# Two attentions on one core: the wait of a split maximum moves into the matmul itself, and row loads go two a step

## The chip, the core and the metric

The kernel runs on one core of a Trainium2 chip. The metric is the device time of one execution in microseconds (us), the median of several runs; lower is better. A core has a matrix engine (PE in the profile; its weight loads are listed apart as PEld), a vector engine (DVE), a scalar engine (ACT), a general engine (POOL), and SP, which here only issues DMA transfers. Each engine takes its instructions in the order in which the program lists them for it, and waits for others through semaphores.

## The reference

Two independent attention layers on inputs of 2048 rows and 576 columns, 32 heads of 18 columns each, results side by side. B, the second, is full softmax attention and makes up nearly all the work; A, the first, looks only at 8 earlier rows (0, 2, ... 14 back).

```python
S, D, H, Dh = 2048, 576, 32, 18
qkv = (x @ wqkv).reshape(S, 3, H, Dh)               # for A and for B
# B: every row against every row
scores = einsum("hqd,hkd->hqk", q, k) * Dh ** -0.5
out_B = einsum("hqk,hkd->hqd", softmax(scores), v) @ wo
# A: row s against rows s, s-2, ..., s-14
logits = where(idx >= 0, einsum("hsd,hswd->hsw", q, k[idx]) * Dh ** -0.5, -1e9)
out_A = einsum("hsw,hswd->hsd", softmax(logits), v[idx]) @ wo
```

## The kernel before, in words

First, up to about 420 us, both projections are computed and stored to DRAM; B's queries and keys go to `dqk`, split into a high and a low part for accuracy. Then the main loop does B's attention while POOL works through A between the lines.

B's heads are taken in 8 groups of 4. For each group, the queries (`qs`) and keys (`ks`) of the four heads are laid into one of three sets of SBUF tiles, so that two heads can share the array: one head stands on partitions 0 to 63 (row group 0), its neighbour on 64 to 127 (row group 1). Matmuls on different row groups run side by side. The softmax needs each row's largest score before the exponential, so every score is computed twice: once, ahead of time, for its row maximum (`take`, line 239; DVE reduces it on lines 256, 258 and 272 into `mx`), and once transposed for the exponential (`score`, line 388; ACT makes the exponentials `e` and `ee` on lines 398 and 401). The maxima of a block go through a small chain (`least`, `turn`, `halve`, `order`, `place`) and through DRAM (`dm`, lines 300 and 306) into two extra rows of `qs`.

The main loop has 512 steps: 8 groups, 4 blocks of 512 queries, 16 blocks of 128 keys. A step's instructions on PE are in a fixed order. In a plain step, `PLAIN = "D1AzwE2B"` gives it, one letter for one matmul:

- `D` and `E`: the two halves (256 columns each) of a maximum in two parts. `D` is on row group 0, `E` on row group 1, and both write into the same bank of PSUM, which one reduction (line 272) then empties. `first_part` issues `D` and hands back a function that issues `E`.
- `A` and `B`: whole maxima (512 columns) on row groups 0 and 1.
- `1` and `2`: scores of heads 1 and 2, on row groups 1 and 0, each in a bank of its own, each emptied by one ACT instruction on line 398.
- `z` and `w`: scores of heads 3 and 0, on row groups 1 and 0, into a tile of two banks (`pair`), emptied by one ACT instruction on line 401.

After these eight, `weigh` (line 870) multiplies the exponentials of the step before with the values into `po`: four matmuls that the profile lists as eight, on all 128 rows of the array. About one step in fifteen also holds products of A's output (line 1211); its order is then made by `in_turn`.

Banks are handed out in turn from two rings: two banks for `1` and `2`, three for `D`, `A` and `B`. So `2` waits until ACT has emptied the bank of the last `2`, and `B` until DVE has emptied the bank of the last `B`.

`E` must not begin while `D` still writes into the bank that they share. Line 267 sees to that: an instruction that does nothing (`nop`) is put ahead of `E` and made to wait for `D`'s semaphore. With `nofuse=True` it stays an instruction of PE's queue.

Transfers are issued by SP from an agenda: `plan(start, pieces)` enters functions under step numbers, and each step runs its own (`due`). For each group from the fourth on (g = 3 to 7), line 1328 enters the twelve loads of the next set of rows (`stack_loads`: six for `qs`, line 216, then six for `ks`, line 215; 288 KB each), from step 64 (g - 2) + 1 on. Other transfers of the same queue lie among them: the maxima (`dm`), the denominators of the softmax (`den`, `drec`, `rec`, lines 904 to 907), the results (`do`, line 900), and for A the rows (`akv`, `aq`, line 996) and the finished attention (`at`, `ahl`, lines 1090 and 1092) that the products of line 1211 read.

Of the kernel before, what the change touches and what calls it, by code (L numbers as in the profile page):

```python
# [33 lines left out]
STEPS = NB * NT  # L34
# [29 lines left out]
def rows(t, *dims):  # L64

    return bass.AP(tensor=t.tensor, offset=t.offset, ap=[list(d) for d in dims])
# [3 lines left out]
def two_attentions(ctx: ExitStack, tc, xa, wa, woa, xb, wb, wob, out):  # L70
# [5 lines left out]
    nc = tc.nc  # L76
# [18 lines left out]
    def bank(kind=None):  # L95
        r = rings[kind or ring]
        n = min((i for i in r if i not in held), key=lambda i: freed[i]) if ring == "pool" else r[0]
        if ring != "pool":
            r.append(r.pop(0))
        t = (p_bank if n < 5 or projecting else p_pair).tile([128, 512], F32, name=f"bank{n}")  # L100
        if not projecting:
            held[n] = t
        return t
# [53 lines left out]
    def filled(r, ns, t=None):  # L157

        n = held_as(t)
        busy[r] = max(busy[r], 0 if n is None else freed[n] + 165) + ns  # L160

    def emptied(engine, ns, r, t):

        busy[engine] = max(busy[engine], busy[r] + 214) + ns
        n = held_as(t)
        if n is not None:
            del held[n]
            freed[n] = busy[engine] + 100
# [6 lines left out]
    def split_on(engine, hi, lo, raw):  # L175
        engine.tensor_copy(hi, raw)
        engine.tensor_sub(lo, raw, hi)
# [5 lines left out]
    def later(n, f):  # L183
        agenda[step + n].append(f)

    def plan(start, pieces):
        for n, f in pieces:
            agenda[start + n].append(f)
# [18 lines left out]
    def stack_loads(g, *pieces, issue=load):  # L207
        qs, ks = (t.bitcast(F32) for t in sets[g % 3])

        def part(t, base, n, r, i, d, m):  # L210

            at = 64 * r + DH * n + d
            first = dqk[i, base + DH * (4 * g + r) + d]
            if t is ks:
                return lambda: issue(ks[at : at + m], rows(first, (S, m), (2 * DH * S, 2), (1, S)))
            return lambda: issue(qs[at : at + m], rows(first, (S, m), (512, NB), (2 * DH * S, 2), (1, 512)))

        return [part(t, base, n, r, i, d, m) for t, base, parts in ((qs, 0, (0, 0, 1)), (ks, D, (0, 1, 0)))
                for d, m in pieces or ((0, DH),) for n, i in enumerate(parts) for r in range(2)]


    def behind_of(later, *before):

        for b in before:
            tc.add_manual_dep(later.ins, b.ins.name,
                              mybir.DependencyInfo(mybir.DependencyClass.Sync, mybir.DependencyReason.DATA),
                              reason="in order")

    def block(g, b):

        qs, ks = sets[g % 3]
        mx = maxes.tile([128, 2, 2, 4, 6], F32, name="mx", bufs=3)
        left = 2 * 8 * 6
        rest = [[(k, t, p) for k in range(NB) for t in range(4) for p in range(2)] for _ in range(2)]

        def take(ps, r, k, t, p, at, n):

            rows_ = slice(64 * r, 64 * r + 54)
            return nc.tensor.matmul(ps, qs[rows_, b, p, 128 * t : 128 * t + 128],  # L239
                                    ks[rows_, p, 512 * k + at : 512 * k + at + n], start=True, stop=True)  # L240

        def made(n):
            nonlocal left
            left -= n
            if left == 0:
                later(int(projecting), least)

        def whole(r):
            k, t, p = rest[r].pop(0)
            ps = bank()  # L250
            take(ps, r, k, t, p, 0, 512)
            filled(r, 226, ps)

            def reduce():
                if k < 2:
                    nc.vector.tensor_reduce(mx[:, r, p, t, k : k + 1], ps, axis=AX.X, op=ALU.max)  # L256
                else:
                    nc.vector.tensor_reduce(mx[:, r, p, t, 2 * k - 2 : 2 * k], ps.rearrange("q (h n) -> q h n", h=2),  # L258
                                            axis=AX.X, op=ALU.max)
                emptied("DVE", 598, r, ps)  # L260
                made(1 + (k > 1))

            return reduce

        def part(i, k, t, p, r, ps, before=None):
            if before:
                behind_of(nc.tensor.nop(nofuse=True), before)
            ins = take(ps[:, 256 * r : 256 * r + 256], r, k, t, p, 256 * i, 256)
            filled(r, 120, None if before else ps)

            def reduce():
                nc.vector.tensor_reduce(mx[:, :, p, t, 2 * k - 2 + i], ps.rearrange("q (h n) -> q h n", h=2),  # L272
                                        axis=AX.X, op=ALU.max)
                emptied("DVE", 598, r, ps)
                made(2)

            return ins, reduce

        def least():
            m = least_rooms[n_least[0] % 2]  # L280
            n_least[0] += 1
            nc.vector.tensor_reduce(m[:, :16], mx.rearrange("q r p t k -> q (r p t) k"), axis=AX.X, op=ALU.max,
                                    negate=True)
            later(1, lambda: turn(m))

        def turn(m):

            parts = maxes.tile([128, 2, 32], F32R, name="mt", bufs=2)
            raw = parts[:, 1].bitcast(F32)
            nc.vector.transpose(raw, m)  # L290
            later(1, lambda: halve(parts, raw))

        def halve(parts, raw):
            split_on(nc.gpsimd, parts[:, 0], parts[:, 1], raw)
            later(1 if g == NG - 1 else 2, lambda: order(parts))

        def order(parts):

            for k in range(2):
                load(rows(dm[g, b, k, 0, 0], (32, 4), (128, 32), (1, 32)), parts[:, k].bitcast(F32))  # L300
            later(1 if g == NG - 1 else 3, place)

        def place():
            placed.add((g, b))
            for k in range(2):
                load(qs.bitcast(F32)[54 + k : 128 : 64, b].rearrange("r p n -> r (p n)"),
                     dm[g, b, k, :16].rearrange("(r i) n -> r (i n)", r=2))

        return rest, whole, part
# [198 lines left out]
    with (tc.tile_pool(name="x", bufs=1, side="right") as xp,  # L508
# [103 lines left out]
        if True:  # L612
# [195 lines left out]
            for k in range(2, 14):  # L808
                n = 46 if k == 2 else 36 + 4 * k
# [7 lines left out]
            def leave_a(c, b, n, ps):  # L817
                o = xp.tile([128, 512], F32, name="ohi", bufs=4)
                nc.scalar.activation(o[:n], ps, AF.Copy)  # L819
                load(da[128 * c : 128 * c + n, HALO + 512 * b : HALO + 512 * b + 512], o[:n])  # L820
# [18 lines left out]
            for c, b in order:  # L839
                n = min(128, 3 * D - 128 * c)  # L840
                work_list.append(((b % 2, ws[c][0], xas[b][0], slice(0, n), every),
                                  lambda ps, n=n: ps[:n], lambda ps, c=c, b=b, n=n: leave_a(c, b, n, ps)))
# [417 lines left out]
    def first(t, b, h):  # L1260
        sums[t, b, h] = bank()
        for c in range(4):
            some(sums[t, b, h][:, :288], t, h, c, *olds[b][c], c == 0, False)
# [44 lines left out]
    def partial(t, h):  # L1308

        b = NB - 1  # L1310
        if h == 0:
            name = ("aq", "ao", "aohi")[t]
            ys["part", t] = work.tile([128, DH, SUB], F32, name=name, bufs=1)
        y = ap(ys["part", t], (1, DH * SUB))[:, 288 * h : 288 * h + 288]
        waiting.append(lambda: alone(*sum_of(y, t, h, olds[b])))
        sums[t, b, h] = (y,)
# [8 lines left out]
        plan(A_FROM + GAP * j, local(j))  # L1325
    for g in range(1, NG):
        if g > EARLY:
            plan(STEPS * (g - 2) + 1, [(n, f) for n, f in enumerate(stack_loads(g))])
        if g == NG - 1:
            plan(STEPS * g, [(4, lambda: fetch_old(0)), (24, lambda: fetch_old(1)), (34, lambda: fetch_old(3)),  # L1330
                             (36, lambda: fetch_old(2))])
            plan(STEPS * g, [(n, lambda t=t, h=h: partial(t, h)) for n, (t, h) in
                             zip((40, 41, 42, 44, 46, 48), [(t, h) for t in range(3) for h in range(2)])])
            plan(STEPS * g, [(62, lambda: outside.append(lambda: first(3, NB - 1, 0)))])
            for b in range(NB - 1):
                producing.update(STEPS * g + NT * (b + 1) + (31 if b == 0 else 7) + n for n in range(8))
        plan(STEPS * (g - 1), [(24, lambda g=g: load_v(g))])
# [19 lines left out]
    while step < ALL:  # L1357
        n, kt = divmod(step, NT)
        g, b = divmod(n, NB)
# [84 lines left out]
```

## Time and profile before

| | |
|---|---|
| time, median of 3 runs | 1599.24 us (1596.97 to 1600.29) |
| the profiled execution | 1598.7 us, its span 1596.8 us |
| granted clock of PE | 0.999 of full speed |
| PE busy | 1586.8 us, 99% of the span |
| DVE, ACT, POOL busy | 88%, 74%, 60% |
| reductions of maxima in two parts (line 272) | 478 |
| loads of rows issued by SP for g = 3 to 7 | 60, of 288 KB |

The span runs from the first to the last instruction. Start times below count from its start. Records of matmuls overlap: one can begin before its weights are all loaded, and the ends are modelled. Weight loads have records of their own, and a matmul's wait for a semaphore stands at its weight load. The records of an instruction that only waits are not counted as busy.

### The profile page before, as it was taken

The page shows a single profiled execution, that of the slowest core. Times are in us where ns is not written, and L with a number is a line of the kernel's source. Part 1 is how long each engine was busy: PE and PEld are TensorE (multiplying, and loading weights), DVE is VectorE, ACT ScalarE, POOL GpSimd, SP SyncE. Part 2 cuts the span into 40 slices and gives each one's busy share as a digit, 9 for nine tenths or more (in the row PEclk, how much of TensorE's full clock was granted, in tenths as well). Part 3 has the DMA queues.
Part 4 walks back from the last instruction along what each step waited for, and adds up shares of the span by engine and source line. Part 5 has one row for each costly group of instructions (what it writes and reads, how often), then busy time and mean ns, then how long its engine had stood idle before and what let it go on. Part 6 is the DMA issues. An engine that isn't in the chain of part 4 may idle for free.

```text
span 1596.8 us, 35241 instructions
## 1 busy us (share of the span) xinstructions
PE 1586.8 (99%) x13436; PEld 931.4 (58%) x13436; DVE 1400.1 (88%) x2381; ACT 1181.3 (74%) x1912; POOL 961.1 (60%) x816
## 2 busy tenths in 40 slices
PE   9999999999999999999999999999999999999998
PEld 7999998888544434444444444444444444445776
DVE  5299999999999989999999999999999999999433
ACT  6324432121699999999999999999999998988444
POOL 2306742210167996994995985995995997940100
PEclk9999999999999999999999999999999999999999
DMA  8948954532321252254236325323623232234211
GB/s 257 230 135 214 273 159 131 137 106 76 66 58 53 57 120 85 73 118 121 59 71 160 78 69 140 95 52 97 132 70 89 70 86 78 60 122 159 85 38 61
DMA packets 190151, 173.15 MB, mean 108 GB/s; under 512 B 123120, under 2 KB 136944, under 8 KB 188256
## 3 DMA queue, kind: packets, MB, share of 16 engines
q1 hardware_dynamic: 185120, 159.36, 36.2%
q0 software_dynamic: 4032, 10.63, 3.2%
q8 instruction: 107, 1.75, 0.5%
q10 hardware_dynamic: 832, 0.92, 0.2%
q14 instruction: 60, 0.49, 0.1%
HBM read 97.47 MB, written 72.95 MB: 107 GB/s over the span
## 4 chain that ended last, share of the span: by engine, by line
PE 93%; POOL 3%; DMA 2%; DVE 1%; issue 0%; SPq 0%; ACT 0%; POOLq 0%; ACTq 0%; DVEq 0%
PE po L870 29%; PE bank L239 20%; PE bank L491 16%; PE bank L388 10%; PE bank L1211 8%; PE pair L388 6%; PE bank L424 4%; POOL pr L1062 1%; DMA ks<-dqk 1%; DMA qs<-dqk 1%; POOL pr L1064 1%; DVE mx L256 0%; PE bank L643 0%; POOL pr L1066 0%; DVE mx L272 0%
## 5 line engine op out<-in xcount | busy, mean ns | idle before, releaser
L239 PE MATMUL bank<-ks,qs 54*128 54x256 f32 (+1 forms) x2526 | 767.1, 377 | 2.3 <-DMA ks<-dqk 1.3
L256 DVE TENSOR_REDUCE mx<-bank 128x1 f32<-128x512 f32 x1024 | 679.5, 683 | 71.2 <-PE bank L239 50.9
L398 ACT ACTIVATE e<-bank 128x512 f32<-128x512 f32 x1024 | 611.6, 602 | 81.8 <-PE bank L388 64.5
L239 PEld LDWEIGHTS bank<-ks,qs 54*128 54x128 f32 x2526 | 398.5, 184 | 459.9 <-DVE mx L272 315.2
L870 PE MATMUL po<-ee,v 128*19 128x512 f32 x2048 | 537.6, 600 | 1.0 <-DVE o L880 0.2
L870 PE MATMUL po<-e,v 128*19 128x512 f32 x2048 | 532.3, 600 | 0.0
L401 ACT ACTIVATE ee<-pair 128x1024 f32<-128x1024 f32 x478 | 487.4, 1020 | 0.9 <-PE pair L388 0.3
L388 PE MATMUL bank<-qs,ks 56*128 56x512 f32 x1092 | 459.7, 441 | 0.0
L258 DVE TENSOR_REDUCE mx<-bank 128x2 f32<-128x512 f32 x546 | 356.3, 683 | 21.9 <-PE bank L239 11.4
L272 DVE TENSOR_REDUCE mx<-bank 128x2 f32<-128x512 f32 x478 | 325.7, 681 | 0.0
L388 PE MATMUL pair<-qs,ks 56*128 56x512 f32 x956 | 248.7, 396 | 0.0
L388 PEld LDWEIGHTS bank<-qs,ks 56*128 56x128 f32 x1092 | 193.8, 183 | 14.5 <-ACT e L398 8.0
L1062 POOL TENSOR_TENSOR pr<-lg,akv 128x1024 f32<-128x1024 f32 x72 | 157.1, 2202 | 0.6
L819 ACT ACTIVATE ohi<-bank 128x512 f32<-128x512 f32 (+1 forms) x56 | 30.4, 595 | 156.0 <-issue 110.7
L388 PEld LDWEIGHTS pair<-qs,ks 56*128 56x128 f32 x956 | 138.5, 186 | 0.0
L870 PEld LDWEIGHTS po<-ee,v 128*19 128x19 f32 x2048 | 69.6, 96 | 113.1 <-issue 109.3
L491 PE MATMUL bank<-xhi,ahi 64*128 64x512 f32 (+1 forms) x448 | 114.4, 390 | 0.0
L491 PE MATMUL bank<-xhi,alo 64*128 64x512 f32 (+1 forms) x448 | 109.0, 390 | 0.0
L491 PE MATMUL bank<-xlo,ahi 64*128 64x512 f32 (+1 forms) x448 | 102.9, 391 | 0.1
L1014 POOL TENSOR_TENSOR pr<-aq,akv 128x1024 f32<-128x1024 f32 x40 | 87.8, 2201 | 18.2 <-PE po L870 16.9
L1064 POOL TENSOR_TENSOR pr<-pr 128x512 f32<-128x512 f32 x72 | 91.2, 1289 | 0.6
L539 POOL TENSOR_TENSOR alo<-raw,ahi 128x512 fp32r<-128x512 f32 (+1 forms) x14 | 17.5, 1254 | 116.3 <-ACT ahi L538 116.3
(206 smaller groups left out, 2370.9 us busy)
## 6 DMA issues: line engine op xcount, KB each, us to landing
do<-n SPq DMA_DIRECT2D x28, 512.0 KB
da<-ohi SPq DMA_DIRECT2D x52, 256.0 KB
akv<-da SPq DMA_DIRECT2D x64, 175.5 KB
out<-y SPq DMA_DIRECT2D x32, 288.0 KB
qs<-dqk SPq DMA_DIRECT2D x30, 288.0 KB
ks<-dqk SPq DMA_DIRECT2D x30, 288.0 KB
at<-dao SPq DMA_DIRECT2D x64, 128.0 KB
rec<-drec SPq DMA_DIRECT2D x29, 256.0 KB
```

Of the source, the lines that this page charges most:

```text
L239: return nc.tensor.matmul(ps, qs[rows_, b, p, 128 * t : 128 * t + 128], ks[rows_, p, 512 * k + at : 512 * k + at + n], start=True, stop=True)
L256: nc.vector.tensor_reduce(mx[:, r, p, t, k : k + 1], ps, axis=AX.X, op=ALU.max)
L258: nc.vector.tensor_reduce(mx[:, r, p, t, 2 * k - 2 : 2 * k], ps.rearrange("q (h n) -> q h n", h=2), axis=AX.X, op=ALU.max)
L272: nc.vector.tensor_reduce(mx[:, :, p, t, 2 * k - 2 + i], ps.rearrange("q (h n) -> q h n", h=2), axis=AX.X, op=ALU.max)
L388: nc.tensor.matmul(ps, ks[at, p, 128 * kt : 128 * kt + 128], qs[at, b, p], start=True, stop=True)
L398: nc.scalar.activation(e, ps, AF.Exp, scale=SCALE)
L401: nc.scalar.activation(whole, both_scores[0], AF.Exp, scale=SCALE)
L491: nc.tensor.matmul(ps, a, b, start=start, stop=stop)
L870: nc.tensor.matmul(po[32 * i : 32 * i + 19], vs[g][:, kt, 19 * i : 19 * i + 19], es[i], start=kt == 0, stop=kt == NT - 1)
L1062: nc.gpsimd.tensor_mul(at, ap(st["lg"], (0, 2), (SUB, W), (1, SUB)), window(st["v"], n))
L1064: nc.gpsimd.tensor_add(at[:, :, :4], at[:, :, :4], at[:, :, 4:])
L1211: nc.tensor.matmul(sums_[r], a, b, start=i == 0, stop=i == len(both[r]) - 1)
```

## The change

Two edits. In `part`, the `nop` loses `nofuse=True`, so that it is merged into the instruction behind it: the wait for `D` is carried by `E`'s own matmul. In the agenda, the loads of a set of rows are entered under `n // 2` in place of `n`: two a step over six steps, not one a step over twelve.

```diff
         def part(i, k, t, p, r, ps, before=None):
             if before:
-                behind_of(nc.tensor.nop(nofuse=True), before)
+                behind_of(nc.tensor.nop(), before)
             ins = take(ps[:, 256 * r : 256 * r + 256], r, k, t, p, 256 * i, 256)
...
     for g in range(1, NG):
         if g > EARLY:
-            plan(STEPS * (g - 2) + 1, [(n, f) for n, f in enumerate(stack_loads(g))])
+            plan(STEPS * (g - 2) + 1, [(n // 2, f) for n, f in enumerate(stack_loads(g))])
```

On PE the order of the matmuls stays. This is one plain step of the kernel before, from `D` to `weigh`, with the semaphore that each waits for; `bank_...`, `pair` and `po` are PSUM tiles, the rest SBUF tiles:

```order
L239 MATMUL bank_10058<-ks_89,qs_88 128x256 [waits DVE_49]
L388 MATMUL bank_10060<-qs_1584,ks_1585 128x512 [waits Activation_49]
L239 MATMUL bank_10064<-ks_89,qs_88 128x512 [waits DVE_49]
L388 MATMUL pair<-qs_1584,ks_1585 128x512 [waits Activation_49]
L388 MATMUL pair<-qs_1584,ks_1585 128x512
L239 MATMUL bank_10058<-ks_89,qs_88 128x256 [waits PE_49]
L388 MATMUL bank_10075<-qs_1584,ks_1585 128x512 [waits Activation_49]
L239 MATMUL bank_10079<-ks_89,qs_88 128x512 [waits DVE_49]
L870 MATMUL po<-ee_10036,v 19x512
```

The kernel after has the same rows. The list leaves out instructions that only wait and puts their wait on the next row: in the kernel before, `PE_49` in the sixth row is the wait of the `nop` ahead of `E`, in the kernel after it is `E`'s own. PE's queue has 11,995 instructions before and 11,516 after: 479 fewer.

On SP the loads move. This is the place of the first set (g = 3, `qs_88` and `ks_89`), the kernel before with -, the kernel after with +:

```order
-L216 DMA qs_88<-dqk 18x8x512
-L300 DMA dm<-mt 4x32x32 x2
-L904 DMA den<-o 128x1x16
-L216 DMA qs_88<-dqk 18x8x512 x3
-L306 DMA qs_3567<-dm 2x1024 x2
 L216 DMA qs_88<-dqk 18x8x512 x2
-L215 DMA ks_89<-dqk 18x2x2048 x3
-L906 DMA drec<-den 128x16
-L215 DMA ks_89<-dqk 18x2x2048
-L900 DMA do<-n 128x2x512
+L300 DMA dm<-mt 4x32x32 x2
+L904 DMA den<-o 128x1x16
+L216 DMA qs_88<-dqk 18x8x512 x4
 L215 DMA ks_89<-dqk 18x2x2048 x2
+L306 DMA qs_3567<-dm 2x1024 x2
+L215 DMA ks_89<-dqk 18x2x2048 x4
+L906 DMA drec<-den 128x16
+L900 DMA do<-n 128x2x512
 L907 DMA rec<-drec 128x1x512
```

All six `ks` loads now stand ahead of `drec` and of the 512 KB of `do`; before, three of them stood behind `drec` and two behind `do`. The transfers of the maxima into `qs` (line 306) stand behind eight loads, before behind four.

The second set (g = 4, `qs_1584` and `ks_1585`) in the kernel before:

```order
L216 DMA qs_1584<-dqk 18x8x512
L904 DMA den<-o 128x1x16
L216 DMA qs_1584<-dqk 18x8x512 x2
L306 DMA qs_88<-dm 2x1024 x2
L216 DMA qs_1584<-dqk 18x8x512
L1151 DMA out<-y 128x576
L216 DMA qs_1584<-dqk 18x8x512 x2
L1090 DMA at_10416<-dao 128x4x64 x2
L1092 DMA ahl<-dao 64x2x64
L1090 DMA at_10420<-dao 128x4x64 x2
L1092 DMA ahl<-dao 64x2x64
L215 DMA ks_1585<-dqk 18x2x2048
```

and in the kernel after:

```order
L216 DMA qs_1584<-dqk 18x8x512 x2
L904 DMA den<-o 128x1x16
L216 DMA qs_1584<-dqk 18x8x512 x4
L306 DMA qs_88<-dm 2x1024 x2
L215 DMA ks_1585<-dqk 18x2x2048 x2
L1151 DMA out<-y 128x576
L215 DMA ks_1585<-dqk 18x2x2048 x4
L1090 DMA at_10422<-dao 128x4x64 x2
L1092 DMA ahl<-dao 64x2x64
L1090 DMA at_10426<-dao 128x4x64 x2
L1092 DMA ahl<-dao 64x2x64
```

Here the six `ks` loads come to stand ahead of the six transfers that bring A's attention (`at`, `ahl`) to the products of line 1211. The third set (g = 5) has the same shift; the last two have none of line 1090's transfers near. No other queue's order of work differs, but for names of buffers.

## The prediction

> **What bounds the kernel now.** I read the page first, then the main loop by windows, then one step in order of time. On the page:
>
> ```profile
> span 1596.8 us, 35241 instructions
> PE 1586.8 (99%) x13436; PEld 931.4 (58%) x13436; DVE 1400.1 (88%) x2381; ACT 1181.3 (74%) x1912; POOL 961.1 (60%) x816
> PE 93%; POOL 3%; DMA 2%; DVE 1%; issue 0%; SPq 0%; ACT 0%; POOLq 0%; ACTq 0%; DVEq 0%
> ```
>
> The third line is the chain that ended last: nearly all PE. The middle of the main loop, by windows, shows two others close behind (DVE 378 and ACT 374 of 400 us):
>
> ```profile
> 800.00:1200.00 400.00, 399.89 (x3286) 181.67 (x3282) 377.81 (x646) 374.23 (x579) 339.24 (x253) 1.00 0.39 97
> ```
>
> The length of a plain step is read from the weight loads of D, in order of time (first and last of nine):
>
> ```profile
> 1121.61 0.18 PEld L239 LDWEIGHTS bank<-ks,qs 54*128 54x128 f32 x1 [0.85 <-DVE mx L272]
> ...
> 1137.89 0.18 PEld L239 LDWEIGHTS bank<-ks,qs 54*128 54x128 f32 x1 [0.85 <-ACT e L398]
> ```
>
> (1137.89 - 1121.61) / 8 = 2.035 us. "Busy" hides what happens inside a step, since the records overlap. One step in order of time (start, length):
>
> ```profile
> 800.24 0.38 PE L239 MATMUL bank<-ks,qs 54*128 54x256 f32 x1
> 800.24 0.49 PE L388 MATMUL bank<-qs,ks 56*128 56x512 f32 x1
> 800.35 0.19 PEld L239 LDWEIGHTS bank<-ks,qs 54*128 54x128 f32 x1
> 800.46 0.39 PE L239 MATMUL bank<-ks,qs 54*128 54x512 f32 x1
> 800.58 0.51 PE L388 MATMUL pair<-qs,ks 56*128 56x512 f32 x2
> 800.74 0.18 PEld L239 LDWEIGHTS bank<-ks,qs 54*128 54x128 f32 x1
> 800.80 0.18 PEld L388 LDWEIGHTS bank<-qs,ks 56*128 56x128 f32 x1
> 800.82 0.31 PE L239 MATMUL bank<-ks,qs 54*128 54x256 f32 x1
> 800.85 0.19 PEld L239 LDWEIGHTS bank<-ks,qs 54*128 54x128 f32 x1
> 800.93 0.39 PE L388 MATMUL bank<-qs,ks 56*128 56x512 f32 x1
> 800.97 0.39 PE L239 MATMUL bank<-ks,qs 54*128 54x512 f32 x1
> 802.10 0.68 DVE L258 TENSOR_REDUCE mx<-bank 128x2 f32<-128x512 f32 x1
> 802.17 0.61 ACT L398 ACTIVATE e<-bank 128x512 f32<-128x512 f32 x1
> 802.27 0.38 PE L239 MATMUL bank<-ks,qs 54*128 54x256 f32 x1
> ```
>
> The matmuls are D, 1, A, z with w (merged), E, 2, B, and the next step's D; the weight loads are those of A, E, 2 and B. The DVE row is B's reduction, the ACT row the exponential of 2. A narrower window shows where w begins:
>
> ```profile
> 800.69 0.40 PE L388 MATMUL pair<-qs,ks 56*128 56x512 f32 x1
> ```
>
> On row group 0, A, w and 2 begin at .46, .69 and .93: one every 0.23 to 0.24, without a hole. On row group 1 there is one: D with its own weight wait lasts 0.38, E 0.31, and a matmul of 256 columns whose weights are ready would last about 0.38 - 0.11 = 0.27 (0.11 is the time from A's weight load, .35, to A's matmul, .46). So E waits 0.04 for its weights, and B begins 0.04 behind 2. Weigh needs the whole array, so the step ends by B: from B's start to the next D 802.27 - 800.97 = 1.30. Those 0.04 are all that PE alone can gain in a step.
>
> **The first edit.** What it removes, by the line's own view:
>
> ```profile
> L267 PEldq EVENT_SEMAPHORE  x478: 51/51/51, 418.3 to 1482.7; - x160
> ```
>
> 478 instructions of 0.051 us each (shortest, median and longest, in ns). D's record ends at 800.62 and E's weight load begins at 800.74: 0.12, of which 0.051 is the nop. What a wait costs that stands at the weight load itself, the load of the next step's 2 shows, which waits for the ACT row above (end 802.17 + 0.61 = 802.78):
>
> ```profile
> 802.83 0.18 PEld L388 LDWEIGHTS bank<-qs,ks 56*128 56x128 f32 x1
> ```
>
> 0.05 after it. Thus E's load should come 0.06 to 0.07 earlier, at about 800.67; the bounds are 0 (a wait for PE's own semaphore could be slower than one for ACT's) and 0.07. Then E's weights are ready at .78, ahead of the end of z's columns (.58 + 0.23 = .81), E starts at .82 without its 0.04, and B comes even with 2.
>
> What is late next: 2 and B wait for banks that ACT and DVE empty a whole step later. With step s at 800.24, the exponential of its 2 ends at 802.78, 2.54 after. The load of 2 in step s+1 follows 0.05 later, its matmul 0.11 (A's) to 0.13 (2's own, .80 to .93) after that, and the step after next begins 1.30 later. Two steps therefore cannot take less than 2.54 + 0.05 + 0.11 + 1.30 = 4.00, or 4.02 with 0.13: 2.00 to 2.01 a step. DVE gives nearly the same: B's reduction ends at 802.10 + 0.68 = 802.78 too. The array alone would allow 2.035 - 0.04 = 1.995. I take 2.008, toward the upper end because the rows are good to 0.01 and the loop through ACT is the closest: 0.027 gained.
>
> How many steps:
>
> ```profile
> L272 DVE TENSOR_REDUCE mx<-bank 128x2 f32<-128x512 f32 x478 | 325.7, 681 | 0.0
> ```
>
> 478 steps have an E; 32 of them hold products of A (8 blocks, 2 halves of rows, 2 of columns), 446 are plain. 446 x 0.027 = 12.0. From that I take a tenth, 1.2, as an estimate: DVE and ACT, 94% busy in the window above, have less room to catch up after the extra work at the end of a block. In the 32 others I take half of 0.06: 1.0. Bounds of the edit: 0, and 446 x 0.04 + 32 x 0.06 = 19.8.
>
> [...]
>
> **The second edit.** The same 60 loads of the same size, issued up to six steps earlier. It matters where a load is waited for. The waits name one place, and the chain shows it:
>
> ```profile
> PE bank L239 <- DMA ks<-dqk: 1.3, 1, 1.3
> ```
>
> ```profile
> 561.50 9.53 DMA qs<-dqk
> 571.10 14.79 DMA ks<-dqk
> ...
> 586.13 0.47 PE bank L239
> ```
>
> The last `ks` load of the first set (g = 3) is issued at 571.10 and lands at 585.89; PE waits 1.3 us for it. SP issues that load late because its queue is full of transfers that have not landed:
>
> ```profile
> 566.74 0.29 SPq L215 DMA_DIRECT2D ks<-dqk  x1
> 567.13 0.39 SPq L900 DMA_DIRECT2D do<-n  x1
> 568.88 2.48 SPq L215 DMA_DIRECT2D ks<-dqk  x2
> ```
>
> The last three `ks` loads go out at 566.7, 568.9 and 571.1: one every 2.2 us, the pace at which 288 KB land. In the kernel after, all six stand ahead of `do`, which is 512 KB, 2.2 x 512 / 288 = 3.9 us of transfer. The last load then lands about 3.9 earlier or better, and the 1.3 is gained whole; between 0 and 1.3. What is pushed back there (`drec`, `do`, `rec`, the two transfers of line 306) feeds POOL's end of a block and maxima that are used blocks later; by the waits, PE waits for none of them. For g = 4 to 7 PE waits for no row load now, so nothing is gained there; what could be lost is the fifth case.
>
> **The sum.** -12.0 + 1.2 - 1.0 - 1.3 = -13.1 us, against the profiled execution's 1598.7 (its span and 1.9 around it): 1585.6. The median is 0.5 higher, 1599.24; less 13.1, 1586.1.
>
> **The rivals.** A measurement of this kernel can tell about 0.2%, 3.2 us, from no change.
>
> 1. The forecast: 1582 to 1590. Chance 0.57.
> 2. ACT's loop holds 2 harder than I think (0.13 and a little more each time): 2.02 a step, 446 x 0.015 = 6.7, 8 or less with the second edit: 1590 to 1596. For it: 2's load already stands as close behind ACT as a load does. Against: B, not 2, is last now. 0.10.
> 3. E's wait is no cheaper in the matmul: only the 1.3 is left, 1597 to 1600. For it: no row shows a weight load behind a wait for a matmul that ran just before. 0.12. [...]
> 4. Neither loop holds: 0.04 a step, with 19.8 + 1.3, about 1578 to 1582. For it: the rows are good to 0.01 only. 0.12.
> 5. Slower: the loads moved ahead of A's attention make PE wait at line 1211. The rows for g = 4:
>
> ```profile
> 699.48 2.91 SPq L1090 DMA_DIRECT2D at<-dao  x2
> 702.44 2.93 SPq L1092 DMA_DIRECT2D ahl<-dao  x1
> ```
>
> ```profile
> 718.67 0.52 PE L1211 MATMUL bank<-wohi,at 64*128 64x288 f32 x4
> ```
>
> The last of them is issued by 705.37 and first read at 718.67: 13.3 us of room. Six `ks` loads ahead at 2.2 each are 13.2, so the issue alone would use up the room, and the landing (14.8 for the load above) would be waited for. It decides once it exceeds 13.3; at worst 14.8 a set. For g = 4 and 5 that is 30 us, less 13: about 1603 to 1616. Against it: at 0.39 the DMA engines are far from full over the window, and `ks` loads that find room are issued in 0.3 us each, 2 us in all. 0.09.
>
> Faster by over 0.2% are cases 1, 2 and 4: 0.79; same is case 3, 0.12; slower 0.09. The range, 1579 to 1598, holds nearly all of 1, 2 and 4 and part of 3, leaving out about 0.15.
>
> **What would show it.** Right: no row for line 267's nop; E's weight load about 0.05 behind D's end, not 0.12; B's matmul level with 2's; D to D 2.00 to 2.01; no wait of PE for `ks`. The loads of 2 and B should then begin right at ACT's and DVE's ends. Wrong: D to D still 2.035 (case 3, or 2 later than w + 0.24, case 2), or a wait of line 1211 for `at` (case 5).

## The result and the profile after

| | before | after |
|---|---|---|
| median | 1598.88 us (1596.97 to 1600.29, 5 runs) | 1589.66 us (1589.29 to 1593.05, 5 runs) |
| profiled execution, its span | 1598.7 us, 1596.8 us | 1589.66 us, 1587.8 us |

The ratio is 0.9951, 95% interval 0.9937 to 0.9966: 9.2 us faster, or 5.4 to 10.1 us by the interval. The forecast was 13.1 us. The page of the kernel after, the lines that answer those of before:

```profile
span 1587.8 us, 34762 instructions
PE 1577.4 (99%) x13436; PEld 971.1 (61%) x13436; DVE 1399.7 (88%) x2381; ACT 1180.6 (74%) x1912; POOL 961.6 (61%) x816
PE 97%; DVE 2%; DMA 1%; issue 0%; ACT 0%; POOL 0%; SPq 0%; ACTq 0%; DVEq 0%; POOLq 0%
```

PE still bounds the kernel: the chain that ended last is 97% PE. There are 479 instructions fewer. The view of line 267 shows one of its 478 instructions left (count, shortest, median and longest in ns, first and last start):

```profile
L267 PEldq EVENT_SEMAPHORE  x1: 51/51/51, 761.6 to 761.6; - x1
```

One step of the kernel after, in order of time (start, length):

```profile
801.58 0.38 PE L239 MATMUL bank<-ks,qs 54*128 54x256 f32 x1
...
802.02 0.18 PEld L239 LDWEIGHTS bank<-ks,qs 54*128 54x128 f32 x1
...
802.16 0.29 PE L239 MATMUL bank<-ks,qs 54*128 54x256 f32 x1
...
802.27 0.41 PE L388 MATMUL bank<-qs,ks 56*128 56x512 f32 x1
802.28 0.40 PE L239 MATMUL bank<-ks,qs 54*128 54x512 f32 x1
...
803.43 0.68 DVE L258 TENSOR_REDUCE mx<-bank 128x2 f32<-128x512 f32 x1
...
804.17 0.18 PEld L388 LDWEIGHTS bank<-qs,ks 56*128 56x128 f32 x1
804.17 0.28 PE L239 MATMUL bank<-ks,qs 54*128 54x256 f32 x1
804.17 0.19 PEld L239 LDWEIGHTS bank<-ks,qs 54*128 54x128 f32 x1
```

The rows are `D`, `E`'s load, `E`, `2`, `B`, then the reduction of this step's `B`, and in the next step the load of `2`, `E`, and the load of `B`. `E`'s load begins 0.06 us behind `D`'s end (801.96), where it was 0.12. `B` begins 0.01 behind `2`, where it was 0.04. `B`'s reduction ends at 804.11, and the load of the next `B` follows 0.06 later: the loop through DVE is closed. A narrower window shows the exponential of `2` on ACT:

```profile
803.51 0.60 ACT L398 ACTIVATE e<-bank 128x512 f32<-128x512 f32 x1
```

It ends at 804.11 too, and the load of the next `2` follows 0.06 later. The length of a step, from the weight loads of `D`:

```profile
1119.54 0.18 PEld L239 LDWEIGHTS bank<-ks,qs 54*128 54x128 f32 x1 [0.85 <-DVE mx L272]
...
1131.57 0.18 PEld L239 LDWEIGHTS bank<-ks,qs 54*128 54x128 f32 x1 [0.85 <-ACT e L398]
1135.67 0.18 PEld L239 LDWEIGHTS bank<-ks,qs 54*128 54x128 f32 x1 [0.85 <-DVE mx L256]
1137.67 0.18 PEld L239 LDWEIGHTS bank<-ks,qs 54*128 54x128 f32 x1 [0.85 <-DVE mx L256]
1139.83 0.18 PEld L239 LDWEIGHTS bank<-ks,qs 54*128 54x128 f32 x1 [0.85 <-DVE mx L272]
```

The first two rows are six steps apart: 12.03 / 6 = 2.005 us. Then come two steps in 4.10, one of 2.00 and one of 2.16: not every step is short. The waits of PE (microseconds in all, times, longest):

```profile
PE bank L643 <- DVE raw L641: 1.5, 1, 1.5
PE bank L1211 <- ACT e L398: 1.0, 1, 1.0
PE bank L239 <- ACT ohi L819: 0.9, 1, 0.9
PE bank L1211 <- DMA at<-dao: 0.5, 1, 0.5
PE bank L1189 <- ACT n L954: 0.3, 1, 0.3
PE po L870 <- DVE o L880: 0.2, 1, 0.2
```

The wait for `ks` is gone, and two waits of line 1211 are new.

**Where the time went.** I split both traces into their 511 steps, each from the first weight load of `weigh` to that of the next `weigh`, and took the differences by class. Differences are after less before, in us:

| class of steps | number | mean before | mean after | sum of differences |
|---|---|---|---|---|
| plain, inside a block | 392 | 2.0391 | 2.0164 | -8.90 |
| last and first step at a block's end | 29 + 29 | 2.067, 2.104 | 2.058, 2.118 | -0.26 + 0.38 |
| with products of A | 33 | 4.1437 | 4.1242 | -0.64 |
| the two at the `ks` wait (g = 3) | 2 | 3.674 | 2.013 | -3.32 |
| the two at the first products of g = 5 | 2 | 3.086 | 4.788 | +3.40 |
| the end of A, and all outside the steps | 24 | | | +0.29 |

The sum is -9.05 of a span that is 9.0 shorter. So the first edit brought about 9.4, and the second, as the kernel stands, nothing: what it gains at g = 3 it loses at g = 5.

**The loss at g = 5.** SP's rows in the kernel after, at the third set:

```profile
831.20 5.34 SPq L215 DMA_DIRECT2D ks<-dqk  x4
838.48 2.65 SPq L1090 DMA_DIRECT2D at<-dao  x2
841.53 3.92 SPq L1092 DMA_DIRECT2D ahl<-dao  x1
845.50 1.13 SPq L1090 DMA_DIRECT2D at<-dao  x2
846.68 4.20 SPq L1092 DMA_DIRECT2D ahl<-dao  x1
```

and the chain that ended last, in which the last of the `at` transfers stands:

```profile
846.14 6.49 DMA at<-dao
```

It lands at 852.63. PE's matmuls there:

```profile
851.87 0.40 PE L1211 MATMUL bank<-wohi,at 64*128 64x288 f32 x2 [0.96 <-ACT e L398]
852.76 0.40 PE L1211 MATMUL bank<-wohi,at 64*128 64x288 f32 x2 [0.49 <-DMA at<-dao]
```

PE stands still for 0.96 and 0.49. The first of these is put down to ACT, the last event before it; no kernel below whose loads of g = 5 keep the old pace has it, so I count it as part of the same delay. The same kernel, run once more below, puts both of its stops (1.1 and 0.4) down to `at`:

```profile
PE bank L1211 <- DMA at<-dao: 1.5, 2, 1.1
```

In the kernel before, SP's rows of the same transfers:

```profile
835.73 3.30 SPq L1090 DMA_DIRECT2D at<-dao  x2
...
844.40 2.87 SPq L1092 DMA_DIRECT2D ahl<-dao  x1
```

and PE's row of that product, in the same kernel:

```profile
857.99 0.49 PE L1211 MATMUL bank<-wohi,at 64*128 64x288 f32 x4
```

The first `at` was issued 22.3 us ahead of the first product (857.99 - 835.73); in the kernel after, 13.4 ahead (851.87 - 838.48).

**Both special places cost more than the wait.** PE waited 1.3 us for `ks` before, and the two steps there were 3.3 longer. It waits 1.45 for `at` now, and the two steps are 3.4 longer. The windows around the two places, of the kernel before (time of each engine, then the granted clock of PE, the DMA share and GB/s):

```profile
584.00:590.00 6.00, 4.67 (x24) 2.04 (x22) 2.56 (x4) 2.81 (x6) 5.92 (x4) 0.72 0.56 116
852.00:858.00 6.00, 6.00 (x51) 2.44 (x48) 6.00 (x12) 5.86 (x10) 0.00 (x0) 1.00 0.62 143
```

and of the kernel after:

```profile
584.00:590.00 6.00, 6.00 (x52) 2.65 (x48) 5.86 (x12) 5.97 (x10) 5.92 (x4) 1.00 0.89 147
852.00:858.00 6.00, 5.50 (x43) 3.65 (x44) 2.98 (x6) 1.50 (x3) 0.00 (x0) 0.72 0.56 196
```

The granted clock is 0.72 over 6 us behind the wait and 1.00 where there is none: 0.28 x 6 = 1.7 us of PE's work. With the waits themselves, 1.33 + 1.7 = 3.0 and 1.45 + 1.7 = 3.1, near the 3.3 and 3.4 measured; the last 0.3 is not explained. The mean clock of the whole execution, 0.999, hides it.

### The profile page after: what moved, and what is told of

It reads as the page before. It is cut to its first block, busy times and chain, and to the rows that moved or that the text cites. A ratio compares the mean times of both kernels' runs of the same rounds, so it can differ in the third digit from the quotient of the medians.

```text
span 1587.8 us, 34762 instructions
## 1 busy us (share of the span) xinstructions
PE 1577.4 (99%) x13436; PEld 971.1 (61%) x13436; DVE 1399.7 (88%) x2381; ACT 1180.6 (74%) x1912; POOL 961.6 (61%) x816
## 4 chain that ended last, share of the span: by engine, by line
PE 97%; DVE 2%; DMA 1%; issue 0%; ACT 0%; POOL 0%; SPq 0%; ACTq 0%; DVEq 0%; POOLq 0%
PE po L870 31%; PE bank L239 20%; PE bank L491 17%; PE bank L388 10%; PE bank L1211 8%; PE pair L388 7%; PE bank L424 4%; DVE mx L256 1%; DMA at<-dao 0%; DVE mx L272 0%; DVE o L880 0%; PE bank L643 0%; DVE mx L258 0%; DMA out<-y 0%; PE bank L1189 0%
## 5 line engine op out<-in xcount | busy, mean ns | idle before, releaser
L239 PE MATMUL bank<-ks,qs 54*128 54x256 f32 (+1 forms) x2526 | 754.6, 372 | 1.0 <-ACT ohi L819 0.9
L239 PEld LDWEIGHTS bank<-ks,qs 54*128 54x128 f32 x2526 | 414.2, 184 | 424.3 <-DVE mx L272 305.0
L258 DVE TENSOR_REDUCE mx<-bank 128x2 f32<-128x512 f32 x546 | 356.5, 684 | 19.5 <-PE bank L239 6.6
L491 PE MATMUL bank<-xhi,ahi 64*128 64x512 f32 (+1 forms) x448 | 120.2, 390 | 0.0
L491 PE MATMUL bank<-xhi,alo 64*128 64x512 f32 (+1 forms) x448 | 114.5, 390 | 0.0
L491 PE MATMUL bank<-xlo,ahi 64*128 64x512 f32 (+1 forms) x448 | 108.8, 391 | 0.1
```

Source lines behind the costliest of these rows:

```text
L491: nc.tensor.matmul(ps, a, b, start=start, stop=stop)
```

## The experiments

The theory after the result: the first edit alone is worth some 9 us; the second gains 3.3 at g = 3 and loses 3.4 at g = 5. The rival for the missing 4 us: the first edit brings all of it and the second only harm, or the second brings its gain and the loops through ACT and DVE hold the first. Where a kernel below is compared by steps, the start up to the first `weigh` is left out: it differed by -0.9 to +9.3 us between profiled executions, in waits that neither edit touches.

### The wait alone, the loads alone

The kernel after with the old pace of the loads:

```diff
-            plan(STEPS * (g - 2) + 1, [(n // 2, f) for n, f in enumerate(stack_loads(g))])
+            plan(STEPS * (g - 2) + 1, [(n, f) for n, f in enumerate(stack_loads(g))])
```

> The first edit alone: the wait stands in E's matmul, the row loads go out one a step as before. Theory: outside the two places where PE waits for a transfer, the first edit is worth 9.1 us (the plain step falls from 2.035 to 2.005); the wait for the last ks load of g = 3 stays and grows by up to the 1.4 us that PE is earlier there; PE does not wait for A's attention in g = 5. So 7 to 9 us below the kernel before, 1590 to 1592. Rival: PE waits for A's attention in g = 5 because PE itself comes earlier, whatever the order of the loads; then that wait is here too, and 3 to 5 us below before is left.

Measured: 1587.89 us (1587.78 to 1589.49, 5 runs) against 1597.53 for the kernel before on that chip, ratio 0.994 (0.9926 to 0.9953). By steps, the plain ones gain 7.84 and those with products 0.57; the two at g = 3 keep 6.78 of their 7.35, with PE's wait and its clock:

```profile
580.00:592.00 12.00, 10.43 (x66) 4.16 (x64) 7.72 (x14) 8.24 (x13) 11.78 (x8) 0.86 0.51 105
```

and the two at g = 5 change by -0.04: that PE comes earlier does not by itself bring the wait for `at`. Of the 1.06 that the plain steps gain less than in the kernel after, 1.03 is a single step, the third behind the stop, which the low clock (0.50 from 586.47 to 589.88) still reaches. So one edit alone gives what both give, and a little more than I expected.

The kernel before with only the new pace of the loads:

```diff
-            plan(STEPS * (g - 2) + 1, [(n, f) for n, f in enumerate(stack_loads(g))])
+            plan(STEPS * (g - 2) + 1, [(n // 2, f) for n, f in enumerate(stack_loads(g))])
```

> The second edit alone: two row loads a step, the instruction that only waits stays. Theory: the wait for ks at g = 3 goes (3.3 us), and A's attention comes late in g = 5, by less than with both edits, since PE arrives there some 4 us later: 0 to 3.3 us below before, the plain step 2.035. Rival: the loads do no harm by themselves, no wait for A's attention: 3.3 below before, clear of noise.

Measured: 1598.33 us (1596.82 to 1603.14, 11 runs), ratio 1.0008 (0.9998 to 1.0018): nothing gained. By steps it gains 3.18 at g = 3 and loses 1.10 at g = 5, with one wait of 0.5 us. The loss is smaller here. The last `at` goes out 3.9 us ahead of the `weigh` that begins the step with the first products (858.89):

```profile
855.03 0.50 SPq L1090 DMA_DIRECT2D at<-dao  x1
```

and the clock stays full:

```profile
855.00:865.00 10.00, 9.37 (x85) 4.75 (x77) 9.46 (x19) 7.50 (x13) 0.00 (x0) 1.00 0.74 191
```

In the kernel after it goes out 2.9 us ahead (846.14 to 849.07); the 0.9 us between them is what PE waits less. That PE comes later, as I expected, is not the reason: the step begins 9.8 us later than in the kernel after, but the first `at` goes out 9.2 later too (847.72, 838.48), so the transfers move with PE. The profiled execution of this kernel would make it 2 us faster but for its start; the runs do not show that.

### The new pace at one set of rows, or at all but one

The kernel after, with the new pace only for the first set:

```diff
-            plan(STEPS * (g - 2) + 1, [(n // 2, f) for n, f in enumerate(stack_loads(g))])
+            plan(STEPS * (g - 2) + 1, [(n // 2 if g == 3 else n, f) for n, f in enumerate(stack_loads(g))])
```

> The first edit, and two loads a step for g = 3 alone; g = 4 to 7 one a step. Theory: both gains without the loss: 9.1 + 3.3 = 12.4 us below before, about 1586.5, no wait for ks at g = 3 and none for A's attention at g = 5. Rival (PE's earlier arrival makes the wait for A's attention): 9 below before, as with both edits.

Measured: 1586.37 us (1585.87 to 1595.37, 6 runs), ratio 0.9942 (0.9921 to 0.9962): 11.2 us under the kernel before on the same chip. By steps: -9.09 in the plain ones, -3.32 at g = 3, -0.05 at g = 5; all steps together, without the start, give -12.7. The runs are 1.2 us short of the 12.4 expected, the steps are not.

The kernel after, with the old pace only at g = 5:

```diff
-            plan(STEPS * (g - 2) + 1, [(n // 2, f) for n, f in enumerate(stack_loads(g))])
+            plan(STEPS * (g - 2) + 1, [(n // 2 if g != 5 else n, f) for n, f in enumerate(stack_loads(g))])
```

> The first edit, and two loads a step for all groups but g = 5. Theory: the loss sits in g = 5 alone, so the time is that of the kernel with g = 3 alone, 12.4 us below before. Rival: moving loads ahead costs a little in g = 4, 6 and 7 too, by contention: 9 to 11 below before.

Measured: 1586.11 us (1585.78 to 1587.81, 5 runs), ratio 0.9927 (0.9913 to 0.994): 11.4 us under the kernel before on the same chip. By steps: -9.08 in the plain ones, -3.16 at g = 3, -0.05 at g = 5, and PE's row for the place has no gap and full clock:

```profile
844.00:864.00 20.00, 20.00 (x182) 11.36 (x184) 19.11 (x37) 16.49 (x29) 5.73 (x10) 1.00 0.64 180
```

All steps together, without the start, give -12.7 here too, so by the steps nothing is lost at g = 4, 6 and 7. The whole loss of the second edit sits at g = 5. The set before it, g = 4, has the same shift and no wait. Its last `at` transfer in the kernel after, on SP in a narrow window:

```profile
705.49 0.50 SPq L1090 DMA_DIRECT2D at<-dao  x1
```

and the first product on PE:

```profile
712.71 0.43 PE L1211 MATMUL bank<-wohi,at 64*128 64x288 f32 x4
```

With the 6.49 that the one at g = 5 took, it would land at 711.98 (an estimate), 0.7 ahead of the product: less than a microsecond of room was left.

### DVE, ACT, or both made shorter

What holds the plain steps at 2.016 on the mean? In the version with the new pace at g = 3 only, DVE's reductions (lines 256, 258, 272) read 384 of the 512 columns of a bank, so their maxima are of fewer scores. Of the three lines, 272:

```diff
-                nc.vector.tensor_reduce(mx[:, :, p, t, 2 * k - 2 + i], ps.rearrange("q (h n) -> q h n", h=2),
+                nc.vector.tensor_reduce(mx[:, :, p, t, 2 * k - 2 + i], ps.rearrange("q (h n) -> q h n", h=2)[:, :, :192],
```

> The kernel with the first edit and two loads a step for g = 3 alone, with shorter reductions: DVE takes the maximum over 384 of the 512 columns of a bank (the maxima are then of fewer scores). PE's and ACT's work is the same. Theory: two loops hold the plain step near 2.005 us, one through ACT to 2's bank, one through DVE to B's bank; with DVE's cut the one through ACT stays, so the median from D to D stays 2.00 to 2.006, with 2's weight load still 0.05 behind ACT's end. The steps at the ends of blocks may gain, in all 1 to 5 us. Rival: DVE alone holds the step; it then falls to 1.995 or below.

Measured: 1579.06 us, ratio 0.9878 (0.9862 to 0.9895). Or ACT's exponentials of a single bank (line 398) over 384 columns; the other 128 columns are not computed, and their tiles, filled with ones once, are kept (not shown in the excerpt):

```diff
-            nc.scalar.activation(e, ps, AF.Exp, scale=SCALE)
+            nc.scalar.activation(*(x[:, : 384 if kind == "single" else 512] for x in (e, ps)), AF.Exp, scale=SCALE)
```

> The same kernel with ACT's single exponentials (of 1 and 2) over 384 of 512 columns; the other columns of their tiles are filled with ones once and kept. DVE's and PE's work is the same. Theory: DVE's loop holds the step, 2.000 to 2.006 from D to D, B's weight load 0.05 behind DVE's end. Rival: ACT alone holds it; it then falls to 1.995 or below.

Measured: 1584.74 us, ratio 0.9916 (0.9901 to 0.9931). Or both:

> Both cuts together. Theory: neither loop holds, and the array alone sets the plain step: 1.995 (2.035 less the 0.04 by which B was behind 2), with 2's and B's weight loads no longer at ACT's and DVE's ends. 392 plain steps at 0.01 less are 4 us, with the ends of blocks 5 to 9. Rival: the array or its issue sets 2.005 already, and the step stays there in all three kernels.

Measured: 1573.69 us, ratio 0.9847 (0.9832 to 0.9861). The durations did fall. The reductions of line 272 in the kernel after (shortest, median and longest, in ns):

```profile
L272 DVE TENSOR_REDUCE mx<-bank x183: 670/682/693, 800.8 to 1199.5; 128x2 f32<-128x512 f32 x183
```

and with both short:

```profile
L272 DVE TENSOR_REDUCE mx<-bank x185: 548/549/554, 800.9 to 1198.6; 128x2 f32<-128x384 f32 x185
```

By steps (median and mean of the plain ones, in us, and the sum for the 58 at a block's end against the kernel before):

| kernel | plain, median | plain, mean | longest tenth from | at block ends |
|---|---|---|---|---|
| before | 2.034 | 2.039 | 2.039 | |
| after | 2.006 | 2.016 | 2.060 | +0.1 |
| DVE short | 2.005 | 2.011 | 2.013 | -3.8 |
| ACT short | 2.004 | 2.012 | 2.018 | +0.2 |
| both short | 2.002 | 2.003 | 2.010 | -5.5 |

With both short the weight loads of `D` stand 14.00 / 7 = 2.000 apart:

```profile
1125.28 0.18 PEld L239 LDWEIGHTS bank<-ks,qs 54*128 54x128 f32 x1 [0.85 <-DVE mx L272]
...
1139.28 0.18 PEld L239 LDWEIGHTS bank<-ks,qs 54*128 54x128 f32 x1 [0.85 <-DVE mx L272]
```

Three things follow. The typical step hardly moves, 2.006 to 2.002, although with both short the loads of `2` and `B` begin 0.11 and 0.44 us behind the last ends of ACT's and DVE's work, on the median, and no longer 0.05 and 0.06: it is at PE's own limit, within 0.004. The 1.995 that I expected with both short did not come; the rival, 2.005 from PE alone, was nearer. Whether the array or the issue of its instructions sets that limit, no run here tells. And the loops show in the other steps: a tenth of the plain steps of the kernel after takes 2.060 and more, a tenth of those with both short 2.010 and more. The mean of the plain steps falls by 0.013, 392 x 0.013 = 5.1 us. At the block ends it is DVE first: with ACT short alone nothing changes there, with both short 1.7 us more than with DVE short.

### The three versions side by side

Both edits, both with the old pace at g = 5, and the wait alone, once more on one chip:

> Both edits, once more, beside the next two on one chip. By the theory that the loads' edit gains 3.3 us at g = 3 and loses 3.4 at g = 5 this and the kernel with the wait's edit alone differ by less than 1 us; if the loss at g = 5 is not in every execution, this is 1 to 3 us faster than that one. It should be 3 to 4 us slower than the kernel whose loads keep the old pace at g = 5.

> Both edits, the loads of g = 5 at the old pace. By the theory the fastest of the three: 0.9922 to 0.9930 of the kernel before, 3 to 4 us under the kernel with both edits. If the first comparison was chance between chips, level with it.

> The wait's edit alone. By the theory level with both edits to 1 us, 0.994 to 0.995 of the kernel before; 3 us above the kernel whose loads keep the old pace at g = 5.

Measured, against 1596.76 us for the kernel before: both edits 1590.76 us (1588.36 to 1594.23, 7 runs), ratio 0.996 (0.9944 to 0.9975); old pace at g = 5 1586.7 us (1586.14 to 1587.75, 5 runs), ratio 0.9937 (0.9924 to 0.995); the wait alone 1589.54 us (1588.3 to 1590.45, 5 runs), ratio 0.9951 (0.9937 to 0.9965). The version with the old pace at g = 5 beats the kernel after by 4.1 us, and no run of the one reaches the range of the other. The wait alone is 1.2 us better than both edits: a little outside the microsecond that I expected, with ranges that overlap; the profiled executions without their starts are 0.2 us apart (-9.0 the wait alone, -9.2 both edits). The 0.9937 lies a little above the 0.9922 to 0.9930 expected. By steps the repeated kernels agree with the first: +3.48 at g = 5 with both edits, -0.04 in the other two.

## Why the prediction was right, and where its sum was off

The range held the time and the sign was right, by the mechanism forecast. Some of that was luck: the range is 19 us wide, the time stands at the upper edge of the forecast's own case (1582 to 1590), and one of the signs named for being wrong, a wait of line 1211 for `at`, did appear. The steps of the prediction:

- **The price of the nop.** Right. `E`'s load was expected 0.06 to 0.07 earlier; by the records it starts 42 ns behind the event that it waits for, where it was 105 ns. A wait for PE's own semaphore was as cheap as one for ACT's (42 ns too). The third case, in which the wait is no cheaper in the matmul, did not happen. Every kernel here keeps the wait for `D`; what `E` would do without it, no run shows.
- **The length of a plain step.** Right in size, 2.006 for 2.008, but not for the reason given. I put the array alone at 1.995 and let the loops hold the step at 2.00 to 2.01. With both loops loosened the step is 2.002: PE itself holds it, and the loops add 0.004 to the typical step. The 0.04 by which `B` was late was rather 0.035 (the median over all plain steps, 0.007 now), and I subtracted the rounded figure.
- **The number of steps times the gain.** This term was mis-sized: 12.0 less 1.2, where the plain steps and the block ends gave 8.9 - 0.1 = 8.8. The typical step gains 0.028, but the mean of the 392 plain ones only 0.0227, since more of them than before run into the loops. The loads of `2` and of `B` now come right at the end of ACT's and DVE's work, so that a delay there lengthens a step (with both engines' work short the mean of the plain ones was 2.003, not 2.016). The tenth that I took off was about right for the block ends, which gave nothing, and missed the steps inside the blocks. With both engines' work short, plain steps and block ends together give 14.0 + 5.5 = 19.5. That this is close to the upper bound of 19.8 is chance: 5.5 at 58 block ends is more than 58 x 0.04 = 2.3, so part of it is time that DVE and ACT cost there in the kernel before too.
- **The product steps.** 1.0 forecast, 0.6 measured.
- **The `ks` wait.** Gained whole, as forecast, but worth 3.3, not 1.3: I counted the wait in the row and not the clock behind it. The windows of the profile before show it (0.72 at 584 to 590); I read only wide ones, such as the one from 800 to 1200, where the clock is 1.00.
- **The fifth case.** It came true for g = 5, on a smaller scale: 3.4 us, not 30 less 13 (the lower of its two times, 1603, is not worked out there). I checked the room at g = 4 alone (13.3 us) and spoke of g = 5 as if it were the same. The rows of before give 10.7 there (844.40 + 2.87 to 857.99). It was also wrong to treat it as a case that excludes the forecast: it came beside it.

The forecast's 13.1 against 9.05 in the profiles: the first edit 2.4 short (11.8 to 9.4), the second 1.4 short (1.3 to a loss of 0.1), and 0.3 outside the steps. The two errors of the second edit, a gain set 2.0 too small and a loss of 3.4 left out, partly cancel in the sum; the kernels with the new pace at g = 3 alone, or at all but g = 5, show each by itself.

## What to carry to other kernels

The wait that stood as an instruction of its own took 0.051 us at each of its 478 passes here; with the wait on the instruction that needs it, that instruction began 0.06 us earlier, of which 0.028 reached the typical step. When a queue of transfers is reordered, compare the room of every reader that stands behind the moved ones, at each place and not at one: 2.6 us less room at g = 5 than at g = 4 cost the whole gain of the edit. And when a step is brought level with two other engines, take the gain from the mean of the steps: here it was 0.0227 us in a plain step, where the typical one gained 0.028, since DVE and ACT, which now come just in time, took part of it back.

## What was not expected of the hardware

Short stops of PE cost more than their length here. At the two places of this argument, PE's wait by its rows and then the lengthening of the steps there were 0.5 and 1.1 us (loads alone, g = 5), 1.33 and 3.3 (before, g = 3), 1.4 and 3.8 in three steps (wait alone, g = 3), 1.45 and 3.4 (after, g = 5). Behind the last three the clock was 0.50 for one stretch of 3.41 us, which is 1.7 us of PE's work each time. The rows of the kernels before, with the wait alone, and after:

```profile
586.52:589.93 3.41, 3.41 (x17) 1.51 (x16) 1.20 (x2) 0.62 (x2) 3.41 (x3) 0.50 0.48 105
586.47:589.88 3.41, 3.41 (x19) 1.27 (x17) 2.04 (x4) 2.11 (x3) 3.38 (x2) 0.50 0.67 140
853.66:857.07 3.41, 3.41 (x24) 2.29 (x25) 1.84 (x3) 1.30 (x3) 0.00 (x0) 0.50 0.53 192
```

Behind the stop of 0.5 it stayed at 1.00, in the row from 855 to 865 above.

The clock of 0.50 came behind stops of 1.33 to 1.45 us in all; a longer one did not always bring it. In the start of the kernel with ACT short, PE stood still for 2.67 us:

```profile
77.50 0.47 PE L239 MATMUL bank<-ks,qs 54*128 54x512 f32 x1 [2.67 <-issue]
```

and the clock stayed at 1.00:

```profile
75.00:80.00 5.00, 2.50 (x35) 2.54 (x37) 1.43 (x3) 0.00 (x0) 0.00 (x0) 1.00 0.96 365
```

What in PE's work around the stop makes the difference, no run here shows.
